# One of twelve streamed weight blocks is loaded over eight DMA engines in place of sixteen

## The chip, the cores and the metric

The kernel runs on one core of one Trainium2 chip. The core has a matrix engine (PE, with its weight loads shown apart as PEld), three elementwise engines (DVE, ACT, POOL), a queue engine (SP), and 16 DMA engines that all DMA queues share. The metric is device time in microseconds of one execution; lower is better. The kernel before takes 1960.46 us (median of three runs, 1957.11 to 1960.54).

## The reference: what is computed

Two independent parts, side by side in the last axis of the output. The weights and inputs are bf16.

```
# part A: attention over segments of 32 tokens with 8 memory rows that are carried along
for s in range(64):                                   # 2048 tokens / 32
    h = concat([mem, x[:, 32*s:32*s+32]])             # 40 rows of 1024
    q, k, v = h @ Wq, h @ Wk, h @ Wv                  # 32 heads of 128, so 1024 -> 4096 each
    p = softmax(where(mask, q @ k.T * 128**-0.5, -1e9))
    o = (p @ v) @ Wo                                  # 4096 -> 1024
    mem, out[s] = o[:8], o[8:]
# part B: a long convolution of u (2048 x 1024) with a kernel built from A, B, C, dt (128 states)
K = einsum('dn,dnl,dn->dl', C, exp(dt*A*l), dt*B).real
y = irfft(rfft(u) * rfft(K)) + u * Dskip
```

Each segment of part A needs the memory that the segment before it made, so the 64 segments run strictly one after the other, and each needs all four weight matrices, 32 MB in all. These do not fit on the chip.

## The kernel before

Part B runs first (about the first 600 us), with preparations for part A beneath it. Then comes the loop over the 64 segments (`for s in range(NS)`, L406), then one last product for the left-over rows (L656 to L670).

**Weight blocks.** A block is 128 rows (partitions) by 2048 bf16 columns, 512 KB, 4096 bytes in each partition. Wq, Wk and Wv have 16 blocks each, (matrix, chunk of 16 heads, one of eight slices of the 1024 inputs); Wo has 16, ("o", u), with two heads in each. Most stay in on-chip memory for the whole loop (`W_res`). Three are parked in other places (`KEPT`). Twelve are streamed: they are loaded again in every segment. They are listed by `STREAM` and `STREAM_O` (L26, L27): k chunk 0 block 2, q chunk 0 block 2, k chunk 1 blocks 1 and 5, q chunk 1 block 4, v chunk 0 blocks 2 and 7, v chunk 1 blocks 4 and 7, and o 4, 8 and 13. That is also the order of their use in a segment, so o 13 is the last of the twelve.

**Where they come from.** Before the loop, `streamed_copies` (L63) makes a private copy of each streamed block in DRAM (tiles `WD_k_...`, `WD_q_...`, `WD_v_...`, `WD_o_...`) of 128 rows by 2048 columns, by one DRAM to DRAM DMA for each (L69). The copies are issued one by one from SP inside part B (L1272).

**How they are loaded.** `unit(key)` (L300) hands out the block that a matmul needs. For a streamed block it calls `stage` (L337), which issues one DMA on SP's queue into one of four slots of the staging tile `wst` (`SLOTS = 4`, slots taken in turn). SP's instruction stream has nothing else in the loop, so it runs ahead of PE: the load of a block is issued as soon as PE has done with the block four places before it, which had the same slot. The first three loads are issued before the loop (L1709). ACT's queue has the small transfers: per segment one load of 128 KB (`PKd`, L376), one of 112 KB (`VXd`, L382), and two stores of 64 KB (`OLd`, L392, and the output rows, L396).

**Who uses them.** In `quads` (L407) each block of q, k or v is used by four matmuls into four column groups (L414). In `oproj` (L520) each block of Wo is used by eight matmuls (L527): blocks 0 to 4 first, then 5 to 7, then 8, 10, 12, 14, 9, 11, 13, 15. After block 13 comes only 15, then the output rows are turned (L627) and become the memory rows of the next segment (`hT`, L629).

**After the loop** the three streamed blocks of Wo are loaded once more (L647) for the last product, ahead of the left-over rows (`OLd`, L652), which are copied into place (L573) for the matmuls of L664.

The DMA semaphores count one step for each DMA engine that a transfer uses. Loads with other shapes that the prediction speaks of: `xb` (L121, 96 partitions of 2048 bytes), and the loads of `Kx` and `Kp` into `XM` and `k` in part B (L1095, 128 partitions of 1024 bytes).

Of the kernel before, what the change touches and what calls it, by code (L numbers as in the profile page):

```python
# [10 lines left out]
BF16 = mybir.dt.bfloat16  # L11
# [13 lines left out]

STREAM = {("k", 0): (2,), ("q", 0): (2,), ("k", 1): (1, 5), ("q", 1): (4,), ("v", 0): (2, 7), ("v", 1): (4, 7)}  # L26
STREAM_O = (4, 8, 13)  # L27

BANK = {("k", 0): "b0", ("q", 0): "b1", ("k", 1): "b2", ("q", 1): "b0", ("v", 0): "b3", ("v", 1): "b2"}
KEPT = {("k", 0, 7): (("K7a", 0, 512), ("K7b", 512, 512), ("K7c", 1024, 512), ("K7d", 1536, 384), (None, 1920, 128)),  # L30
# [28 lines left out]
def streamed_keys():  # L59
    return [key for key in [(m, t, kc) for (m, t), kcs in STREAM.items() for kc in kcs] + [("o", u) for u in STREAM_O]]  # L60


def streamed_copies(ctx, tc, src):  # L63
    nc = tc.nc
    dram = ctx.enter_context(tc.tile_pool(name="a_wd", bufs=1, space=bass.MemoryType.DRAM))
    out, copies = {}, []
    for key in streamed_keys():
        t_ = dram.tile([128, 2048], BF16, name="WD_%s" % "_".join(str(i) for i in key))
        copies.append(lambda t_=t_, key=key: nc.sync.dma_start(  # L69
            out=t_[:].rearrange("e (h d) -> e h d", h=2) if key[0] == "o" else t_[:], in_=src(key)))  # L70
        out[key] = t_
    return out, copies


class Ahead:
# [3 lines left out]
    def __init__(self, ctx, tc, x, src, seg_len):  # L79
        self.nc, self.tc, self.x, self.src = tc.nc, tc, x, src  # L80
        self.S, self.Dm = x.shape
        self.SL, self.XM = seg_len, 24
        self.XL, self.KC, self.NS = seg_len - 24, self.Dm // 128, self.S // seg_len
        dram = ctx.enter_context(tc.tile_pool(name="a_dram", bufs=1, space=bass.MemoryType.DRAM))
        self.VXd = dram.tile([self.NS + 1, 128, 256 + self.KC * self.XM], BF16, name="VXd")
        self.PKd = dram.tile([self.NS, 128, 512], BF16, name="PKd")
        self.PVd = [dram.tile([self.NS * self.XL, 2048], BF16, name="PVd%d" % t) for t in range(2)]
        self.OLd = dram.tile([self.NS // 8, 128, 8 * 256], BF16, name="OLd")
# [183 lines left out]
def part_a(ctx, tc, x, src, WD, HE, seg_len, out_a, ahead, W_res, rest, places, first):  # L272
    nc = tc.nc
# [26 lines left out]
    def unit(key):  # L300
        if key in rest:

            rest.remove(key)
            load_resident(tc, wres, src, key, W_res, None, places.pop(0)() if places else None)
        if key in W_res:
            return W_res[key]
        if key in KEPT:
            return ahead_of.pop(key) + halves.get(key, [])
        between.pop(key, lambda: None)()
        if key in first:  # L310
            return first.pop(key)
        if key[0] == "v":
            for k_ in rest[0:3 if key[1] == 0 else 1]:
                rest.remove(k_)
                load_resident(tc, wres, src, k_, W_res)
        return stage(key, WD[key][:])

    ctx_l = ctx_w.enter_context(ExitStack())
    pers = ctx_l.enter_context(tc.tile_pool(name="a_pers", bufs=1))
# [14 lines left out]
    def words(out, in_):  # L334
        nc.vector.tensor_scalar(out=out.bitcast(I32), in0=in_.bitcast(I32), scalar1=0, scalar2=None, op0=ALU.bitwise_or)  # L335

    def stage(key, in_):  # L337
        t_ = wst.tile([128, 2048], BF16, name="wst", tag="w%d" % (loads[0] % SLOTS))
        loads[0] += 1
        nc.sync.dma_start(out=t_[:].rearrange("e (h d) -> e h d", h=2) if len(in_.shape) == 3 else t_[:], in_=in_)  # L340
        return t_

    def load_kept(key):
# [62 lines left out]
    for s in range(NS):  # L406
# [123 lines left out]
        a = quads("k", 0, (0, 2, 4, 6, 1, 3, 5, 7))  # L530
        k0 = evac(a, "k0")
        a = quads("q", 0, range(0, 6))
# [4 lines left out]
        a = quads("k", 1, range(0, 3))  # L537
# [16 lines left out]
        a = quads("q", 1, range(KC))  # L554
# [3 lines left out]
        a = quads("v", 0, range(0, 3))  # L558
# [34 lines left out]
        a = quads("v", 1, range(0, 5))  # L593
# [46 lines left out]
    wo = {}  # L640
    for u in order:
        if ("o", u) in W_res:
            wo[u] = W_res["o", u]
        else:
            wo[u] = spare.pop(0)
            if ("o", u) in WD:
                nc.sync.dma_start(out=wo[u][:], in_=WD["o", u][:])  # L647
            else:
                nc.sync.dma_start(out=wo[u][:].rearrange("e (h d) -> e h d", h=2), in_=src(("o", u)))
    stores(NS - 1, ob)  # L650
# [6 lines left out]
    for b in range(4):  # L657
        pe = [ps_k.tile([128, 512], F32, name="pe", tag="keep%d" % (2 * (b % 2) + n)) for n in range(2)]
        for u in order:
            for hh in range(2):  # L660
                h = 2 * u + hh
                hi = 16 * (h // 16) + 4 * (h % 4) + (h % 16) // 4
# [983 lines left out]
@with_exitstack  # L1646
def kernel(
    ctx: ExitStack,
    tc: tile.TileContext,
    A_x: bass.AP,  # L1650
    A_mem0: bass.AP,
    A_Wq: bass.AP,
    A_Wk: bass.AP,
    A_Wv: bass.AP,
    A_Wo: bass.AP,
    A_seg_len: bass.AP,
    B_u: bass.AP,
    B_A_re: bass.AP,
    B_A_im: bass.AP,
    B_B_re: bass.AP,  # L1660
    B_B_im: bass.AP,
    B_C_re: bass.AP,
    B_C_im: bass.AP,
    B_log_dt: bass.AP,
    B_Dskip: bass.AP,
    out: bass.AP,
):
    seg_len = int(A_seg_len)
    Dm = A_x.shape[2]
    Db = B_u.shape[2]  # L1670
    out_a = out[0, :, 0:Dm]
    out_b = out[0, :, Dm:Dm + Db]
    src = weight_blocks(A_Wq.rearrange("d h e -> d (h e)"), A_Wk.rearrange("d h e -> d (h e)"),
                        A_Wv.rearrange("d h e -> d (h e)"), A_Wo.rearrange("h e d -> (h e) d"))
    WD, copies = streamed_copies(ctx, tc, src)
    ahead = Ahead(ctx, tc, A_x[0], src, seg_len)
    ctx_w = ctx.enter_context(ExitStack())
    W_res, places, first = {}, [], {}
    rest = Keys(RESIDENT)
    rest.ctx = ahead.ctx = ctx_w  # L1680

    def residents(stay, early, uqs, last):
        def put(t_):
            load_resident(tc, None, src, rest.pop(0), W_res, None, t_)
        for _ in range(EARLY[0]):
            load_resident(tc, stay, src, rest.pop(0), W_res)
            yield
        def some(where, tag, n):
            t_ = where.tile([128, n, 2048], BF16, name="W%d" % n, tag=tag)
            return [t_[:, i, :] for i in range(n)]  # L1690
        for t_ in some(stay, "KT1", 2):
            put(t_)
            yield
        for t_ in early:
            put(t_)
            yield
        put(last[0])
        yield
        for t_ in uqs:
            put(t_)  # L1700
            yield
        ahead.wst = ctx_w.enter_context(tc.tile_pool(name="a_wst", bufs=1, side="right"))
        pool = ctx_w.enter_context(tc.tile_pool(name="a_wre0", bufs=1, side="right"))
        for _ in range(EARLY[1]):
            load_resident(tc, pool, src, rest.pop(0), W_res)
            yield
        for i, key in enumerate([("k", 0, 7)] + streamed_keys()[0:SLOTS - 1]):
            first[key] = t_ = ahead.wst.tile([128, 2048], BF16, name="wst", tag="w%d" % i)
            tc.nc.sync.dma_start(out=t_[:], in_=WD[key][:] if key in WD else src(key))  # L1709
            yield  # L1710
        for i in [c // 2 for c in PAIRS]:
            places.append(lambda i=i: stay.tile([128, 2048], BF16, name="W1", tag="MI%d" % i))
        for i in range(LATE):
            put(places.pop(0)())
            yield
        put(last[1])
        yield

    low = low_blocks(ctx, tc)
    ahead.low = low.pop()  # L1720
    copies += [lambda t_=t_: load_resident(tc, None, src, rest.pop(0), W_res, None, t_) for t_ in low]

    def first_state(m0, xt):
        nc = tc.nc
        consts = constants(tc, ahead)
        hT = next(consts)
        nc.sync.dma_start(out=xt[:].rearrange("p k r -> p (k r)"), in_=ahead.VXd[0, :, 256:])
        nc.sync.dma_start(out=m0, in_=A_mem0[0])
        pm = yield
        for kc in range(8):  # L1730
            nc.tensor.transpose(out=pm[:, kc, :], in_=m0[:, kc * 128:(kc + 1) * 128], identity=ahead.consts[0][0:8, 0:8])
        nc.vector.tensor_copy(out=hT[:, :, ahead.XM:], in_=pm)
        nc.gpsimd.tensor_copy(out=hT[:, :, 0:ahead.XM], in_=xt[:])
        yield
        next(consts)
        yield

    with ExitStack() as ctx_b:
        part_b(ctx_b, tc, B_u[0], B_A_re, B_A_im, B_B_re, B_B_im, B_C_re, B_C_im, B_log_dt, B_Dskip, out_b, ahead, copies, residents, first_state)
    with ExitStack() as ctx_a:  # L1740
        part_a(ctx_a, tc, A_x[0], src, WD, A_Wo.shape[0] * A_Wo.shape[1], seg_len, out_a, ahead, W_res, rest, places, first)
# [35 lines left out]
```

## Time and profile before

| | us |
|---|---|
| median of three runs | 1960.46 (1957.11 to 1960.54) |
| profiled execution, span from first to last instruction | 1954.2 |
| part B and preparations | about 0 to 612 |
| loop over 64 segments | about 612 to 1890 |
| last product | about 1894 to 1954 |

| engine | busy us in the whole span | share |
|---|---|---|
| PE | 1810.2 | 93% |
| PEld | 1106.9 | 57% |
| DVE | 1379.4 | 71% |
| ACT | 934.7 | 48% |
| POOL | 443.1 | 23% |

PE's granted clock is full in the loop. The DMA engines moved 591.08 MB, 302 GB/s over the span. Four groups make up 768 of the DMA issues: the streamed loads of v (256), k (192), o (192) and q (128), 512 KB each.

How to read it: matmuls are pipelined and their ends are modelled, so a busy PE is not PE at its peak. The DMA share is the mean over 16 engines of the time in which they have a packet in work. A wait is put down to what ended last before the waiting instruction. A row of the chain of waits has the start, the duration and what it was; its DMA pieces run from the issue to the landing.

### The profile page before, as it was taken

To read this page: it belongs to the slowest core of one execution; us is meant where nothing else is said; L and a number is where in the kernel's file an instruction comes from. 1 tells how busy PE (TensorE), PEld (TensorE's weight loads), DVE (VectorE), ACT (ScalarE), POOL (GpSimd) and SP (SyncE) were. 2 spreads that over 40 slices of the span, in tenths; PEclk is the share of its full clock that TensorE was granted. 3 is DMA by queue.
4 is the path that set the end of the run, shared out by engine and by line. 5 is a ranking of instruction groups with operands and counts; after the bars stand their busy time and mean duration, and the time that the engine had idled before them with its cause. 6 is when DMAs were issued, how large, how long until landed. Compare 5 with 4: busy or idle time off the path is not lost.

```text
span 1954.2 us, 74192 instructions
## 1 busy us (share of the span) xinstructions
PE 1810.2 (93%) x31750; PEld 1106.9 (57%) x31788; DVE 1379.4 (71%) x3431; ACT 934.7 (48%) x1670; POOL 443.1 (23%) x855
## 2 busy tenths in 40 slices
PE   8999999887997899999999999999999999998998
PEld 3666666556775555555555555555555555555554
DVE  8599989889994566666676766676766676666650
ACT  8799989851122334344434443444444444444320
POOL 2364545223222111111111111111111111111120
PEclk8999999878998999999999999999999999999999
DMA  7889898867589999999999999999999999999991
GB/s 222 243 232 283 237 287 243 221 188 253 169 272 334 347 340 340 340 339 336 355 339 346 345 335 336 339 341 350 344 350 334 347 341 347 339 350 324 338 343 30
DMA packets 337342, 591.08 MB, mean 302 GB/s; under 512 B 94848, under 2 KB 211048, under 8 KB 334964
## 3 DMA queue, kind: packets, MB, share of 16 engines
q1 hardware_dynamic: 284824, 531.85, 79.9%
q10 hardware_dynamic: 45532, 29.57, 4.9%
q0 software_dynamic: 6656, 24.92, 3.5%
q8 instruction: 249, 4.08, 0.8%
q14 instruction: 81, 0.66, 0.1%
HBM read 528.78 MB, written 68.47 MB: 306 GB/s over the span
## 4 chain that ended last, share of the span: by engine, by line
PE 37%; DMA 27%; DVE 4%; issue 1%; ACT 1%; POOL 0%; SPq 0%; ACTq 0%; DVEq 0%; POOLq 0%
PE acc L414 20%; DMA wst<-WD_v 8%; PE pp L527 8%; DMA wst<-WD_o 7%; DMA wst<-WD_k 3%; DMA arena<-PKd 3%; DMA wst<-WD_q 3%; PE pe L664 3%; PE tr L425 2%; DMA out_dram<-arena 1%; DMA out_dram<-uu 1%; PE pv L495 1%; PE pv L499 1%; DVE arena L621 1%; PE sc L439 1%
## 5 line engine op out<-in xcount | busy, mean ns | idle before, releaser
L414 PEld LDWEIGHTS <-a_hT 128*32 128x32 bf16 x12352 | 328.4, 96 | 324.0 <-issue 64.0
L420 ACT CAST arena<-acc 128x512 bf16<-128x512 f32 x384 | 224.8, 585 | 404.3 <-PE acc L414 324.5
L414 PE MATMUL acc<-wst,a_hT 128*32 128x512 bf16 x2304 | 229.5, 382 | 34.2 <-DMA wst<-WD_v 22.9
L527 PEld LDWEIGHTS <-arena 128*32 128x32 bf16 x8256 | 216.1, 96 | 73.2 <-issue 49.3
L335 DVE TENSOR_SCALAR arena<-keep 128x256 int32<-128x256 int32 (+1 forms) x512 | 175.6, 395 | 28.1 <-PE acc L414 28.0
L428 POOL COPY arena<-arena 128x128 bf16<-128x128 bf16 x128 | 37.3, 292 | 683.0 <-DMA arena<-PKd 314.4
L414 PE MATMUL acc<-XM,a_hT 128*32 128x512 bf16 x2560 | 172.7, 380 | 0.0
L458 ACT ACTIVATE sc<-sc 128x160 f32<-128x160 f32 (+1 forms) x192 | 63.9, 333 | 127.6 <-DVE sc L455 127.6
L454 DVE TENSOR_REDUCE a_mx<-sc 128x4 f32<-128x160 f32 (+1 forms) x192 | 71.7, 374 | 74.7 <-PE sc L442 73.3
L197 PE MATMUL pro<-XM,wsl 128*128 128x512 bf16 x480 | 117.7, 383 | 5.3 <-DVE kst L206 2.2
L527 PE MATMUL pp<-W_o,arena 128*32 128x256 bf16 x3584 | 120.6, 273 | 0.1
L414 PE MATMUL acc<-W,a_hT 128*32 128x512 bf16 x1536 | 120.0, 384 | 0.0
L542 DVE COPY arena<-tr 128x512 bf16<-128x512 bf16 x64 | 27.2, 425 | 128.8 <-PE tr L425 128.8
L462 DVE TENSOR_REDUCE a_mx<-sc 128x4 f32<-128x160 f32 (+1 forms) x192 | 72.9, 379 | 55.3 <-ACT sc L458 54.9
L489 POOL TENSOR_TENSOR arena<-arena,a_BD 128x128 bf16<-128x128 bf16 x128 | 51.1, 399 | 231.1 <-DVE arena L472 229.7
L1266 DVE TENSOR_SCALAR nr<-ptt 128x456 f32<-128x456 int16 x128 | 80.4, 628 | 31.8 <-PE ptt L1244 29.0
L1258 ACT ACTIVATE E<-pa 128x648 bf16<-128x648 f32 x128 | 87.7, 712 | 18.1 <-PE pa L1250 16.0
L414 PE MATMUL acc<-wq,a_hT 128*32 128x512 bf16 x1024 | 92.2, 381 | 0.0
L414 PE MATMUL acc<-g,a_hT 128*32 128x512 bf16 x1024 | 90.4, 379 | 0.0
L1459 POOL TENSOR_TENSOR Bt<-ev 128x512 bf16<-128x512 f32 x32 | 55.7, 1760 | 150.2 <-DVE ev L1456 150.2
L621 ACT CAST arena<-pp 128x128 bf16<-128x128 f32 x64 | 17.0, 265 | 149.8 <-DVE arena L621 149.8
L425 PEld LDWEIGHTS <-arena 128*128 128x128 bf16 x1024 | 57.8, 98 | 54.4 <-issue 45.1
(339 smaller groups left out, 4071.3 us busy)
## 6 DMA issues: line engine op xcount, KB each, us to landing
wst<-WD_v SPq DMA_DIRECT2D x256, 512.0 KB
wst<-WD_k SPq DMA_DIRECT2D x192, 512.0 KB
wst<-WD_o SPq DMA_DIRECT2D x192, 512.0 KB
wst<-WD_q SPq DMA_DIRECT2D x128, 512.0 KB
Ud<-ux POOLq DMA_DIRECT2D x16, 1024.0 KB, 8.2
wq<-Ud SPq DMA_DIRECT2D x32, 512.0 KB
wsl<-in_A_Wk_dram SPq DMA_DIRECT2D x16, 512.0 KB
wsl<-in_A_Wv_dram SPq DMA_DIRECT2D x16, 512.0 KB
```

The lines of the kernel that those rows point to most:

```text
L197: nc.tensor.matmul(a[:], lhsT=w[:, kc, 128 * j:128 * j + 128], rhs=xTl[:, kc, :, :].rearrange("p s k -> p (s k)"), start=(kc == 0), stop=( ...
L335: nc.vector.tensor_scalar(out=out.bitcast(I32), in0=in_.bitcast(I32), scalar1=0, scalar2=None, op0=ALU.bitwise_or)
L414: nc.tensor.matmul(a[32 * g:32 * g + 32, o_:o_ + rhs.shape[1]], lhsT=hT[:, kc, :], rhs=rhs, start=(kc == 0), stop=(kc == KC - 1), tile_pos ...
L420: nc.scalar.copy(out=q, in_=a[:])
L425: nc.tensor.transpose(out=p[:, hl, :, :].rearrange("p a b -> p (a b)"), in_=q[:, 128 * hl:128 * hl + 128], identity=ident[:])
L454: nc.vector.tensor_reduce(out=m_, in_=x, axis=AX.X, op=ALU.max)
L458: nc.scalar.activation(out=flat(sc, i), in_=flat(sc, i), func=ACT.Exp, scale=scale)
L462: nc.vector.tensor_reduce(out=m_, in_=x, axis=AX.X, op=ALU.add)
L527: nc.tensor.matmul(po[32 * qt:32 * qt + 32, o_:o_ + rhs.shape[1]], lhsT=oT[:, h % 4, (h % 16) // 4, :], rhs=rhs, start=False, stop=(h == 3 ...
L664: nc.tensor.matmul(pe[n][:], lhsT=left[2 * b + hi // 16][:, 128 * (hi % 16):128 * (hi % 16) + 128], rhs=wo[u][:, 1024 * hh + 512 * n:1024 ...
L1258: sc.activation(out=T["E", r, e // 4][:, lo:lo + 8 * NE].rearrange("p (i c) -> p i c", i=2), in_=T.pop(("p", r, e))[:, :, 0:4 * NE], func= ...
L1266: v.tensor_scalar(out=T["n", r, e // 4][:, lo:lo + 8 * NT], in0=T.pop(("t", r, e))[:, 0:8 * NT].bitcast(I16)[:, 0:16 * NT:2], scalar1=floa ...
```

## The change

Block o 13 gets another layout in its private DRAM copy and another access pattern in its loads. Its copy is now a tile of 8 rows, each holding 16 of the 128 weight rows (64 KB) and a gap of 64 elements (128 bytes) behind them, so that the 8 rows can't be read as one run. A load reads it as 8 x 16 x 2048 where it read 128 x 2048, so its slowest dimension is 8: the transfer goes over eight DMA engines, 16 rows each, and not over sixteen with 8 rows each. The DMA that fills the copy has that form too. The other eleven blocks keep their layout, their loads and their order. The same loads are issued at the same places of the program (in `stage`, after the loop, and before it), now through a small class. The data and the arithmetic are the same.

```diff
+PORTIONS = {("o", 13): ((128, 8),)}
...
+PITCH = 64
...
+class Streamed:
+    def __init__(self, dram, nc, src, key):
+        self.nc, self.src, self.key, self.pieces = nc, src, key, []
+        lo = 0
+        for i, (rows, engines) in enumerate(PORTIONS.get(key, ((128, 16),))):
+            name = "WD_%s_%d" % ("_".join(str(j) for j in key), i)
+            each = rows // engines
+            if key in PORTIONS:
+                t_ = dram.tile([engines, each * 2048 + PITCH], BF16, name=name)
+                ap = t_[:, 0:each * 2048].rearrange("a (b f) -> a b f", f=2048)
+            else:
+                ap = dram.tile([128, 2048], BF16, name=name)[:]
+            self.pieces.append((lo, lo + rows, ap))
+            lo += rows
+        assert lo == 128
+    def copy(self):
+        for lo, hi, ap in self.pieces:
+            flat = ap if len(ap.shape) == 2 else None
+            w = self.src(self.key)[lo:hi]
+            if self.key[0] == "o":
+                w = w.rearrange("(a b) h d -> a b h d", a=ap.shape[0]) if flat is None else w
+                out = ap.rearrange("a b (h d) -> a b h d", h=2) if flat is None else ap.rearrange("e (h d) -> e h d", h=2)
...
+            self.nc.sync.dma_start(out=out, in_=w)
+    def load(self, t_):
+        for lo, hi, ap in self.pieces:
+            self.nc.sync.dma_start(out=t_[lo:hi, :], in_=ap)
...
 def streamed_copies(ctx, tc, src):
...
+    out = {key: Streamed(dram, tc.nc, src, key) for key in streamed_keys()}
+    return out, [w.copy for w in out.values()]
...
-        return stage(key, WD[key][:])
+        return stage(key)
...
-    def stage(key, in_):
+    def stage(key):
         t_ = wst.tile([128, 2048], BF16, name="wst", tag="w%d" % (loads[0] % SLOTS))
         loads[0] += 1
-        nc.sync.dma_start(out=t_[:].rearrange("e (h d) -> e h d", h=2) if len(in_.shape) == 3 else t_[:], in_=in_)
+        WD[key].load(t_)
         return t_
...
-                nc.sync.dma_start(out=wo[u][:], in_=WD["o", u][:])
+                WD["o", u].load(wo[u])
```

More of the change, by code (lines that the diff above doesn't have):

```diff
@@ L60, in streamed_keys @@
     return [key for key in [(m, t, kc) for (m, t), kcs in STREAM.items() for kc in kcs] + [("o", u) for u in STREAM_O]]
+PITCH = 64
[21 more added lines that the diff above has]
+                out = ap.rearrange("a b (h d) -> a b h d", h=2) if flat is None else ap.rearrange("e (h d) -> e h d", h=2)
+            else:
+                w = w.rearrange("(a b) f -> a b f", a=ap.shape[0]) if flat is None else w
+                out = ap
+            self.nc.sync.dma_start(out=out, in_=w)
+    def load(self, t_):
+        for lo, hi, ap in self.pieces:
+            self.nc.sync.dma_start(out=t_[lo:hi, :], in_=ap)
 def streamed_copies(ctx, tc, src):
-    nc = tc.nc
     dram = ctx.enter_context(tc.tile_pool(name="a_wd", bufs=1, space=bass.MemoryType.DRAM))
[L66 to L72, printed above, removed]
+    out = {key: Streamed(dram, tc.nc, src, key) for key in streamed_keys()}
+    return out, [w.copy for w in out.values()]
 class Ahead:
@@ L1708, in residents @@
             first[key] = t_ = ahead.wst.tile([128, 2048], BF16, name="wst", tag="w%d" % i)
-            tc.nc.sync.dma_start(out=t_[:], in_=WD[key][:] if key in WD else src(key))
+            if key in WD:
+                WD[key].load(t_)
+            else:
+                tc.nc.sync.dma_start(out=t_[:], in_=src(key))
             yield
```

## The prediction

> **What bounds the kernel now.** I read the page's slices first, then the stretch of the loop (about 612 to 1890 us, 64 segments), the queues in it, the chain of waits, and the waits for the staging tile.
>
> The slices of the page, forty of 48.9 us; the loop is slices 13 to 39:
>
> ```profile
> DMA  7889898867589999999999999999999999999991
> GB/s 222 243 232 283 237 287 243 221 188 253 169 272 334 347 340 340 340 339 336 355 339 346 345 335 336 339 341 350 344 350 334 347 341 347 339 350 324 338 343 30
> ```
>
> Busy time by stretch, for the whole loop and for one segment (PE, weight load, DVE, ACT, POOL, clock, DMA share, GB/s):
>
> ```profile
> 612.00:1890.00 1278.00, 1199.16 (x25539) 698.49 (x25540) 839.61 (x2618) 524.57 (x1149) 201.49 (x513) 0.99 0.96 342
> 1201.75:1221.66 19.91, 18.77 (x403) 10.92 (x402) 12.95 (x41) 8.20 (x19) 2.77 (x8) 1.00 0.93 329
> ```
>
> PE and the 16 DMA engines are both nearly full. Two and a quarter segments in the queue view (packets, MB, share of 16 engines) and its rate in forty slices of 1.125 us:
>
> ```profile
> GB/s 404 386 293 362 299 396 375 323 379 348 389 251 280 262 284 266 317 360 397 353 335 351 376 374 403 389 348 362 321 269 310 353 284 328 353 317 386 350 330 354
> ...
> q1 hardware_dynamic: 3915, 14.24, 88.0%
> q10 hardware_dynamic: 1385, 0.93, 6.5%
> q8 instruction: 8, 0.13, 1.2%
> q14 instruction: 2, 0.02, 0.1%
> ```
>
> The chain of waits in the same stretch, in order of time, and PE's idle time before matmuls of the staging tile, over the whole run (us, times):
>
> ```profile
> 1204.36 6.49 DMA wst<-WD_v
> ...
> 1222.32 7.23 DMA wst<-WD_q
> ...
> 1235.97 6.51 DMA wst<-WD_k
> ```
> ```profile
>   DMA wst<-WD_v: 22.9, 25
>   DMA wst<-WD_o: 8.8, 18
>   DMA wst<-WD_k: 6.4, 11
>   DMA wst<-WD_q: 4.3, 6
> ```
>
> The chain runs from a released slot through a 6 to 7 us load back to a matmul. Shown waits are only 42.4 us (0.66 us a segment) because the four slots pace themselves: each load is issued when PE frees the slot of four blocks before. I set the landing of each load (the semaphore steps, one for each DMA engine it uses) against the first matmul of its block, segments 5 to 61. Block 13 is issued, lands 5.32 us later (the fifteenth of its 16 engines after 4.93), and is used 0.15 us after landing; in 74% of segments within 0.2 us. No other block of the twelve has so little room (k1 of chunk 1 has 0.69 us, o 4 has 0.24). So what is added to block 13's landing goes to PE almost whole.
>
> The trace also has a record of every DMA packet. Between 700 and 1800 us a 4096-byte packet takes 159 ns in the median, the next on its engine starts 155 ns after it began, and the mean is 180 ns. The bound is therefore each engine's own pace, not the sum: slices reach 404 GB/s.
>
> How full is each engine? q1, q10 and the fetches make 95.8% of a 19.9 us segment, 19.1 us for the mean engine. The store of the output rows (L396) shows only four landings of its own, 32 packets of 512 bytes at 27 ns on each of four engines: 0.86 us on these, 0.22 in the mean. These four carry 19.1 + 0.64 = 19.7 us of 19.9, the other twelve some 18.9. Four engines are full, and they are among the eight of the change: at L1095 two loads with four landings each go ahead of one with eight, and of its eight, four land after 2.70 to 3.06 us and four after 5.69 to 6.48, behind the two. [...]
>
> **The change part by part.**
>
> Block 13's load in the loop, 64 times. 512 KB on 16 engines is 8 packets each, 8 x 155 ns = 1.24 us; on eight engines it is 16, 2.48 us. The eight lowest gain 1.24 us a segment, the eight highest lose it. The full four are among the gainers. The relief of the others is worth nothing where a block waits for its last engine.
>
> Do packets keep their pace? Each of eight engines now writes 16 neighbouring partitions. The trace has loads of this shape in small: Kx into XM and k (L1095), 1024-byte packets on four or eight engines, each with 32 or 16 neighbouring rows of the 128. By packet records, 364.5 to 366.5 us, the 1024-byte packets took 46 ns in the median (mean 50). From 488 to 489.25 us, with only such a load in flight, they took 61.5 in the mean (1.34 times 46). From 367 to 369.25 us, beside 16-engine loads of 4096-byte packets, they took 73.5 (1.60 times) and the neighbours 226 (1.42 times 159). So the extra is 0 to 0.60 of 16 x 155 ns = 2.48 us, that is 0 to 1.49 us; I take 0.45, 1.12 us, since the loop always has other loads in flight, as the slower row has, while the first row shows that it need not happen at all.
>
> [...]
>
> Against it I set 0.15 us of block 13's room and 0.15 of the 0.66 us of waits, as a longer stop at block 13 gives the three loads already queued time to land. Per segment 1.24 + 1.12 - 0.15 - 0.15 = 2.06 us; times 64 is 132 us.
>
> The issue on SP. L1095's loads held SP 582 ns in the median where L340's hold it 320, so 0.26 us more. SP's next issue (chunk 0 of k, 1.46 us later in the segment above) waits for a slot of PE's anyway: nothing, or 0.26 x 64 = 17 us if that cover went. Nothing else is queued on SP in the loop.
>
> The copy into the private DRAM tile (L69, at 286 to 317 us). 256 packets of 2048 bytes on eight engines in place of 16, 84 ns each in the row of xb's loads: at most 16 x 84 = 1.3 us more, read first at 636 us; 0 to 1.3, I take nothing. The 128-byte gap between engine shares moves no byte and I price it at nothing.
>
> The last load (L647) lands at 1897.2 us, and its matmuls come at 1903.9. The OLd loads behind it on the same engines move by 1.2 to 2.4 us; the copies made from them end 0.6 us before the second block of the last product starts. 0 to 1.8 us; I take 1.
>
> Sum: 133 us on the profiled 1954.2; the runs shown have a median of 1960.46, 6.3 us above that span. 1960.5 + 133 = 2093 us.
>
> **The rivals.**
>
> Only the packets (no crowding). Speaks for it the 46 ns of the first row. 1.24 - 0.30 = 0.94 us, times 64, plus 1: 2021 us.
>
> [...]
>
> No change. Either memory and not the engines sets the 342 GB/s, so that eight engines run faster while eight rest, or the load still goes over all 16: 1960 us. Against the first, the 155 ns that hardly any packet undercuts and slices of 404; against the second, Kx's third load, of the same form (8 x 16 rows), has eight landings of its own. [...]
>
> Faster. If the eight highest engines were the late ones, their 1.24 us would come off the blocks that wait for them. Half of the 42.4 us of waits is 21: 1939 us. It decides only from the point where the lowest eight have 1.24 us of room a segment; the mean engine has 4.2% of 19.9 = 0.8, and the lowest four 0.2. Speaks for it that the last landing moves about: after an instruction fetch one engine is 1 to 2 us late, and in most of these cases it is not one of the four that store the rows.
>
> **How the numbers follow.** Crowding in part 52% (2093; its own range 2060 to 2135, from factors 1.34 to 1.60 and 0.2 us more or less given back), only the packets 26%, full crowding 8%, no change 7%, faster 7%. The range that leaves out no change, faster and the far end of full crowding, some 18%, is 2000 to 2180. About 0.2% (4 us) is what runs of this kernel can tell from no change: faster 7%, within 6%, slower 87%.
>
> **What would show it.** Block 13's load should have eight landings of its own and eight at once; its landing should come 2 to 2.5 us later, with PE waiting there about 2 us a segment, 64 times; waits for the k and q blocks behind it should shrink. GB/s in the loop should fall to about 310 and the segment grow to some 21.9 us. Packets of 4096 bytes well above 159 ns while block 13 is in flight would confirm the crowding; 159 there would leave only 1.24. It is wrong if PE's wait at block 13 stays under 0.3 us or if the segment keeps 19.8 us.

## The result, and the profile after

The changed kernel takes 2244.09 us (median of four runs, 2227.24 to 2252.33) against 1960.5 us for the kernel before: ratio 1.1439, 95% interval 1.1388 to 1.1489, some 284 us slower. The profiled execution has a span of 2250.6 us (before: 1954.2). Lines have moved: L414 is now L446, L527 is L559, and the streamed loads are issued at L98.

The slices of the page after, forty of 56.3 us: granted PE clock, DMA share, rate.

```profile
PEclk8999998699988899999998989999999999989999
DMA  7989987676998889889888888988898888888992
GB/s 216 256 244 268 266 245 216 208 248 190 292 313 265 265 283 290 272 271 285 287 270 248 259 263 279 285 281 282 278 284 284 285 280 262 277 270 283 294 286 74
```

In the loop the rate is about 280 GB/s where it was 340, and the DMA share is 8 tenths where it was 9: the engines, once nearly full, now stand idle part of the time. The clock digits are the first surprise: the loop's slices show 9 and several 8, where they showed 9 throughout before; a slice with an 8 is a mean of stretches at full and at half clock (the run's clock records are 1.0 and 0.5 alone).

Busy time by stretch after (us; PE, weight load, DVE, ACT, POOL with their instructions; PE clock, DMA share, GB/s): from the first matmul of a staged block to the end of the last, and the first 6.4 us of one segment.

```profile
609.60:2189.70 1580.10, 1300.34 (x25656) 718.20 (x25649) 846.54 (x2633) 525.86 (x1152) 205.31 (x515) 0.92 0.89 279
1323.48:1329.85 6.37, 6.37 (x80) 2.62 (x80) 2.32 (x8) 1.24 (x3) 0.29 (x1) 0.67 0.70 222
```

The same stretch before:

```profile
608.90:1892.90 1284.00, 1203.36 (x25654) 701.24 (x25647) 844.04 (x2632) 525.83 (x1152) 201.80 (x514) 0.99 0.96 342
```

So the loop grew by 296.1 us: PE stands idle 199.1 us longer (279.8 against 80.6), and it is busy 97.0 us longer with the same matmuls. The second row of after shows why it is busy longer: at the start of this segment PE is busy without a break, at a clock of 0.67.

PE's idle time before matmuls of the staging tile after, whole run (us, times), and the costliest groups of PE after, one row for each shape (busy us, mean ns, idle before):

```profile
  DMA wst<-WD_o: 218.4, 99
  DMA wst<-WD_v: 23.0, 24
```
```profile
L446 PE MATMUL acc<-W_k,a_hT 128*32 128x512 bf16 x768 | 98.7, 574 | 0.0
L446 PE MATMUL acc<-Wlow,a_hT 128*32 128x512 bf16 x768 | 98.7, 573 | 0.0
L559 PE MATMUL pp<-wst,arena 128*32 128x256 bf16 x1536 | 80.9, 288 | 228.8 <-DMA wst<-WD_o 218.4 <-DVE arena L367 9.5 <-DVE a_mx L495 0.3
```

Waits for the Wo blocks went from 8.8 to 218.4 us; those for the k and q blocks behind them (6.4 and 4.3) are gone. The matmuls of W_k and Wlow, the first of a segment, took 379 and 383 ns before and take 574 and 573 now. The row of Wlow before:

```profile
L414 PE MATMUL acc<-Wlow,a_hT 128*32 128x512 bf16 x768 | 64.4, 383 | 0.4 <-DVE a_hT L629 0.4
```

One stop in full. PE's timeline after (start, us, operation, in brackets the idle time before it and what ended it), and the chain of waits in the same stretch:

```profile
1315.03 1.26 PE L559 MATMUL pp<-W_o,arena 128*32 128x256 bf16 x40
1321.44 0.62 PE L559 MATMUL pp<-wst,arena 128*32 128x256 bf16 x8 [5.15 <-DMA wst<-WD_o]
...
1323.48 0.62 PE L446 MATMUL acc<-Wlow,a_hT 128*32 128x512 bf16 x4
1323.88 0.65 PE L446 MATMUL acc<-wst,a_hT 128*32 128x512 bf16 x4
...
1327.71 0.41 PE L446 MATMUL acc<-wst,a_hT 128*32 128x512 bf16 x4
```
```profile
1310.48 10.92 DMA wst<-WD_o
1321.40 0.04 issue
1321.44 1.10 PE pp L559 x11
...
1337.36 10.23 DMA wst<-WD_o
```

Block 13 is issued at 1310.48 and lands 10.92 us later; PE is through with the blocks ahead of it at 1316.3 and stands for 5.15 us (the mean is 2.95). Four matmuls of the next segment's first blocks then take 0.62 to 0.65 us, until at 1327.71 the same four take 0.41 again.

The queues in 1300 to 1345 us after (packets, MB, share of 16 engines):

```profile
q1 hardware_dynamic: 2961, 10.86, 78.6%
q10 hardware_dynamic: 808, 0.54, 3.9%
```

Read as time per packet, q1's 78.6% of 16 x 45 us over 2961 packets is 191 ns each; the prediction's rows of before give 88.0% of the same over 3915, 162 ns. Fewer packets fit, and each holds its engine longer.

The records of landings and of single packets say the same for the mean of segments 5 to 61. "At 159" is the share of 4096-byte packets of at most 165 ns, among those of all loads between 1.5 us after block 13's issue and its landing. "Half clock" is the time with a granted clock of 0.5, from the loop's first matmul of a staged block to its last. The rows below the second are the experiments.

| kernel | block 13, issue to landing, us | PE stands before it, us | segment, us | packet in flight, mean ns | at 159 | half clock in the loop, us |
|---|---|---|---|---|---|---|
| before | 5.32 | none | 19.69 | 194 | 89% | 17 |
| after | 9.08 | 2.95 | 24.26 | 254 | 36% | 266 |
| e1 16 engines x 8 neighbouring rows | 7.12 | 0.73 | 20.94 | 232 | 38% | 34 |
| e2 four loads of 8 x 4 | 7.63 | 2.22 | 22.27 | 220 | 55% | 157 |
| e3 two loads of 16 x 4 | 6.35 | 0.38 | 20.27 | 222 | 48% | 20 |
| e4 after, wait filled with matmuls | 8.95 | 0.56 | 23.06 | 248 | 36% | 34 |
| e5 after, wide gap in the copy | 8.92 | 3.08 | 23.85 | 252 | 36% | 241 |
| e6 before, padded copy | 5.36 | none | 19.84 | 191 | 89% | 17 |
| e11 loads of 8 x 12 and 8 x 4 | 8.24 | 2.48 | 23.11 | 226 | 46% | 188 |
| e12 four loads of 16 x 2 | 7.04 | 0.64 | 21.20 | 233 | 44% | 48 |
| e7 before + extra packets, DRAM to DRAM | 6.13 | 0.57 | 20.24 | 180 | 91% | 34 |
| e13 before + extra packets, rows 0 to 63, two loads | 6.04 | 0.74 | 20.47 | 187 | 90% | 38 |
| e14 before + extra packets, rows 64 to 127, two loads | 7.29 | 1.25 | 21.79 | 225 | 47% | 85 |
| e15 before + extra packets, rows 0 to 63, one load | 7.57 | 1.29 | 21.84 | 213 | 50% | 89 |

Block 13's load has sixteen landings before, at 3.36 to 5.32 us after the issue (means), and nine in the changed kernel: one record at 1.04 us, and eight at 6.62 to 9.08 us.

### The profile page after: what moved, and what is told of

Its sections match the earlier page's. It is cut to its first block, busy times and chain, and to the rows that moved or that the text cites. A ratio compares the mean times of both kernels' runs of the same rounds, so it can differ in the third digit from the quotient of the medians.

```text
span 2250.6 us, 74230 instructions
## 1 busy us (share of the span) xinstructions
PE 1910.3 (85%) x31788; PEld 1124.3 (50%) x31788; DVE 1379.8 (61%) x3431; ACT 935.2 (42%) x1670; POOL 445.4 (20%) x855
## 4 chain that ended last, share of the span: by engine, by line
PE 37%; DMA 35%; DVE 1%; issue 0%; ACT 0%; SPq 0%; ACTq 0%; DVEq 0%
PE acc L446 27%; DMA wst<-WD_o 26%; DMA wst<-WD_v 8%; PE pe L696 2%; PE pp L559 2%; PE tr L457 2%; PE tro L659 1%; DVE arena L653 1%; PE sc L471 1%; PE yp L1543 1%; DMA wst<-WD_k 0%; DMA out_dram<-uu 0%; PE hps L1543 0%; DMA a_half<-in_A_Wq_dram 0%; ACT arena L653 0%
## 5 line engine op out<-in xcount | busy, mean ns | idle before, releaser
L446 PEld LDWEIGHTS <-a_hT 128*32 128x32 bf16 x12352 | 336.8, 103 | 392.8 <-issue 137.9
L559 PEld LDWEIGHTS <-arena 128*32 128x32 bf16 x8256 | 222.5, 98 | 301.4 <-issue 277.1
L559 PE MATMUL pp<-wst,arena 128*32 128x256 bf16 x1536 | 80.9, 288 | 228.8 <-DMA wst<-WD_o 218.4
L446 PE MATMUL acc<-wst,a_hT 128*32 128x512 bf16 x2304 | 241.4, 408 | 24.2 <-DMA wst<-WD_v 23.0
L653 DVE CAST arena<-pp 128x128 bf16<-128x128 f32 x64 | 18.6, 291 | 260.7 <-PE pp L559 260.7
L446 PE MATMUL acc<-XM,a_hT 128*32 128x512 bf16 x2560 | 172.4, 381 | 0.0
L229 PE MATMUL pro<-XM,wsl 128*128 128x512 bf16 x512 | 124.4, 387 | 3.7 <-DVE XM L144 2.2
L559 PE MATMUL pp<-W_o,arena 128*32 128x256 bf16 x3584 | 124.0, 277 | 0.5 <-issue 0.5
L446 PE MATMUL acc<-W,a_hT 128*32 128x512 bf16 x1536 | 118.0, 383 | 0.0
L1298 DVE TENSOR_SCALAR nr<-ptt 128x456 f32<-128x456 int16 x128 | 80.3, 627 | 30.5 <-PE ptt L1276 27.5
L446 PE MATMUL acc<-W_k,a_hT 128*32 128x512 bf16 x768 | 98.7, 574 | 0.0
L446 PE MATMUL acc<-Wlow,a_hT 128*32 128x512 bf16 x768 | 98.7, 573 | 0.0
```

Source lines behind the costliest of these rows:

```text
L229: nc.tensor.matmul(a[:], lhsT=w[:, kc, 128 * j:128 * j + 128], rhs=xTl[:, kc, :, :].rearrange("p s k -> p (s k)"), start=(kc == 0), stop=( ...
L446: nc.tensor.matmul(a[32 * g:32 * g + 32, o_:o_ + rhs.shape[1]], lhsT=hT[:, kc, :], rhs=rhs, start=(kc == 0), stop=(kc == KC - 1), tile_pos ...
L559: nc.tensor.matmul(po[32 * qt:32 * qt + 32, o_:o_ + rhs.shape[1]], lhsT=oT[:, h % 4, (h % 16) // 4, :], rhs=rhs, start=False, stop=(h == 3 ...
L653: (nc.scalar.copy if j else nc.vector.tensor_copy)(out=osb[:, 128 * j:128 * j + 128], in_=pp[:, 1, 128 * j:128 * j + 128])
L1298: v.tensor_scalar(out=T["n", r, e // 4][:, lo:lo + 8 * NT], in0=T.pop(("t", r, e))[:, 0:8 * NT].bitcast(I16)[:, 0:16 * NT:2], scalar1=floa ...
```

## The experiments

**Is it the copy's layout?** e5 widens the gap in the changed kernel's copy from 128 bytes to 4224; e6 gives the kernel before a copy whose rows have a gap, still 128 rows over 16 engines.

```diff
-PITCH = 64
+PITCH = 2112
```
```diff
-        t_ = dram.tile([128, 2048], BF16, name="WD_%s" % ...)
+        t_ = dram.tile([128, 2048 + 64 * (key == ("o", 13))], BF16, name="WD_%s" % ...)[:, 0:2048]
```

> The changed kernel with a gap of 4224 bytes in place of 128 behind each engine's 64 KB in the private copy, so that the eight engines read from other offsets. Crowding where the block is written: nothing changes, 2225 to 2255 us. The layout of the private copy slows the reads: the time falls by 50 us or more, towards 2100.

> The kernel before, with 128 bytes behind every row of block 13's private copy; the load reads 128 rows of 4096 bytes over sixteen engines as before. Crowding where the block is written: as before, 1955 to 1970 us. Padded reads are slow: 2000 to 2080 us, as with the sixteen engines of eight neighbouring rows (2039.88).

Measured: e5 2231.54 us, ratio 1.1378 [1.1335, 1.1421]; e6 1957.77, 0.9985 [0.9966, 1.0004]. Neither gap matters, so the price is not in the gaps of the copy but in how the load is shared out.

**What does the unequal share alone cost?** e7 keeps block 13 as it was and puts one DRAM to DRAM transfer of 256 KB over eight engines ahead of it in each segment: eight engines get eight packets more, as in the change, but none of them goes to on-chip memory.

```diff
+        if key == ("o", 13):
+            nc.sync.dma_start(out=extra[0][:, 0:8 * 2048].rearrange("a (b f) -> a b f", f=2048),
+                              in_=WD[key][:].rearrange("(a b) f -> a b f", a=8)[:, 0:8, :])
```

> The kernel before, with one more DMA per segment, issued on SP ahead of block 13's load: 256 KB from DRAM to DRAM over eight engines, 8 packets of 4096 bytes on each, written nowhere on chip and used by nothing. It prices the eight extra packets an engine without the neighbouring rows. Unequal share costs the packets' own time, 1.24 us a segment less 0.3: 2010 to 2050 us. If the share costs nothing until rows crowd: 1960 to 1975 us. If DRAM to DRAM packets take much longer than 155 ns, more than 2050, to be read beside their durations.

Measured: 1991.14 us, 1.0153 [1.0118, 1.0189], +30 us or 0.47 us a segment. This lies between the two expected ranges. 91% of packets stay at 159 ns. Eight packets of 155 ns on "full" engines should have cost 0.94 us by the prediction's sum (1.24 less the 0.30 given back); they cost half of that, and block 13 lands 0.81 us later, not 1.24.

e8 aimed at the same point from the other side: in the kernel before, the store of the output rows, put down to four engines, is cut into four stores.

```diff
-            nc.scalar.dma_start(out=rows, in_=ob[:, 0, :])
+            for q in range(4):
+                nc.scalar.dma_start(out=rows[q], in_=ob[32 * q:32 * q + 32, 0, :])
```

> The kernel before, with the store of the output rows, which uses four engines, cut into four stores over sixteen engines. If four engines are full and pace the loop, as the prediction reads it, the loop loses up to 0.6 us a segment: 1920 to 1950 us. If they don't, or if three more issues on ACT delay its next copy out of PSUM: 1955 to 2000 us.

Measured: 2013.11 us, 1.0287 [1.0256, 1.0318]. This is above both expected ranges, and it says nothing of the four engines: ACT now waits 104.5 us for its stores of OLd before it writes its copies, so the longer queue on ACT spoils the comparison.

**How do other forms of block 13's load do?** Each is one line of the changed kernel, (rows, engines) for each load, in order:

```diff
-PORTIONS = {("o", 13): ((128, 8),)}
+PORTIONS = {("o", 13): ((128, 16),)}            # e1
+PORTIONS = {("o", 13): ((32, 8),) * 4}          # e2
+PORTIONS = {("o", 13): ((64, 16),) * 2}         # e3
+PORTIONS = {("o", 13): ((96, 8), (32, 8))}      # e11
+PORTIONS = {("o", 13): ((32, 16),) * 4}         # e12
```

> Block 13 goes over sixteen engines again, 8 packets each, but in the padded layout, so that each engine may write 8 neighbouring partitions. Crowding (engines that write neighbouring partitions get in each other's way): packets of block 13 slow down though no engine has more of them, its landing moves from 5.3 us to 6 or 7, time 1985 to 2080 us. Unequal share alone (eight extra packets an engine): as before, 1960 us. Layout of the private copy (padded rows read slower): late as well, 1985 to 2080.

> Block 13 goes over the eight engines in four loads of 32 rows, 4 rows an engine in each, so that an engine still has 16 packets but at any time the eight are on eight different groups of 4 partitions. Crowding: most of the delay goes, the landing is 1.2 to 2 us later than before in place of 3.8, time 2010 to 2080 us. Unequal share alone: the packets an engine has are the same, so 2220 to 2260 us. Three further issues on SP at about 0.6 us each should cost nothing, or up to 1.8 us a segment.

> Block 13 goes over sixteen engines in two loads of 64 rows, 4 rows an engine, 8 packets an engine in all, padded layout. [...] Unequal share alone: 1960 to 1970 us. Layout of the copy: like the run with four loads, whatever that one shows.

| form | median us | ratio |
|---|---|---|
| e1, 16 x 8 neighbouring rows | 2039.88 | 1.0405 [1.036, 1.0451] |
| e2, four loads 8 x 4 | 2133.43 | 1.0883 [1.0824, 1.0942] |
| e3, two loads 16 x 4 | 2001.73 | 1.0208 [1.0164, 1.0251] |
| e11, 8 x 12 and 8 x 4 | 2161.91 | 1.1035 [1.0989, 1.1081] |
| e12, four loads 16 x 2 | 2055.84 | 1.0497 [1.0457, 1.0538] |

e1 is the most telling: all 16 engines, 8 packets each as before, only with neighbouring rows on one engine. It costs 80 us, and its packets in flight are at 159 ns only 38% of the time, against 89%. That is crowding without any unequal share, with a somewhat later start of its packets in it (see e9). e2 was a miss: it was expected at 2010 to 2080, as each of its loads spreads eight engines over different rows. The last of the four is issued 2.11 us after the first, which explains part of it, but 45% of its packets are slow too. e3's 2001.73 us lie above the 1960 to 1970 expected of the unequal share alone, and 48% of its packets are at 159 ns.

**Loads by themselves.** e9 and e10 leave the whole computation out and run each form eight times in a row into one tile.

> Leaves out the whole computation: only loads of 4096-byte rows from DRAM into one tile on chip, eight of each form, one at a time, nothing else in flight. Forms (engines x neighbouring rows of each): 16 x 8 as the kernel before reads them, 8 x 16 as in the change, 16 x 8 neighbours as in the run with sixteen, then 2 x 16, 2 x 32, 4 x 16, 8 x 4, 16 x 4. [...] Rival, neighbouring rows are slow only beside other loads: 159 ns in every form. Rival, an engine is slow by itself when it walks over many rows: 2 x 16 slow like 8 x 16.

> Leaves out the whole computation, as the run with loads alone. [...] Rival, slowing grows with the number of rows of an engine or of engines: 8 x 12 and 4 x 24 slow like 8 x 16 or little less.

Measured, 4096-byte packets after each engine's first three (mean ns, share at 159; engines x rows of each). A packet's record doesn't name its engine, which is inferred from the packets' times, so another way to infer it moves some of these shares by up to about ten points. The loads of the first row ran beside the copies that prepare the other forms; the others ran alone.

| form | e9 | e10 |
|---|---|---|
| 16 x 8 as before | 169, 92% | |
| 16 x 8 neighbouring | 231, 25% | |
| 8 x 16 | 205, 36% | 208, 34% |
| 8 x 12 | | 161, 95% |
| 8 x 8 | | 168, 88% |
| 8 x 4 | 159, 100% | |
| 4 x 16, 4 x 24, 4 x 32 | 186, 67% (4 x 16) | 164, 97% (4 x 24); 183, 70% (4 x 32) |
| 6 x 16 | | 177, 75% |
| 2 x 16, 2 x 32 | 172, 92%; 186, 71% | 188, 65% (2 x 32) |
| 16 x 4 | 174, 71% | 169, 81% |

Block 13's form slows its packets with no other form in flight. Neither the number of engines nor that of rows decides: 8 x 12 moves 96 rows at 161 ns and 4 x 24 the same at 164, while 4 x 16 is at 186. So the rival of e10 fails for these two forms. For 2 x 32 the runs differ little (186 and 188 ns). Which forms are clean was not explained, but it led to the guess that e11, made of the two clean forms 8 x 12 and 8 x 4, would run clean in the loop, and that e12 would.

These loads show something else: SP takes longer to issue such a load, and its packets start later. In e9 the issue of an 8 x 16 load takes 567 to 634 ns, and its first packet starts 1.34 us after the issue began (median). The one plain load with nothing ahead of it took 319 ns to issue, and its first packet started after 0.95 us. In the loop block 13's issue takes 599 ns in place of 320 (medians), so some 0.4 us of its later landing is this later start, by an estimate from e9.

> [...] Rival, any neighbouring rows or any load on eight engines is slow: 2200 us or more.

> [...] It prices the three further issues on SP without unequal share or crowding, beside the run with four loads over eight engines (2133.43). Theory: issue at 0.32 us each puts the last quarter some 1 us later, 1980 to 2030 us, so that the rest of that run's 173 us is the unequal share and its longer issues; if the issues cost more than 2 us, 2080 or more and that run said little of crowding.

Measured: 2161.91 us for e11, near the 2200 of its rival, and 2055.84 for e12, between its two ranges, with 46% and 44% of packets at 159. e11's forms, clean alone, are not clean beside the other blocks' loads. So the next guess was that it counts which rows the packets write while other loads are in flight.

**Which rows are written.** To tell this apart, the kernel before keeps block 13's load, and extra loads ahead of it put eight more packets on each of eight engines, always 256 KB, rewriting rows of a resident block with the values they hold. The edit of e13, with e14's and e15's differences:

```diff
+EXTRA = (0, 32)                 # e14: (64, 96)
...
+        if key == ("o", 13):
+            for lo, e_ in extra:     # e_: 8 x 4 rows; e15: one load, 8 x 8 rows, EXTRA = (0,)
+                nc.sync.dma_start(out=W_res["k", 1, 0][lo:lo + 32, :], in_=e_)
```

e13 writes rows 0 to 63, in two loads with four rows an engine in each, e14 rows 64 to 127 in the same form, and e15 rows 0 to 63 again, in one load with eight neighbours an engine. The packet records name neither engine nor row, so which engine writes which row is not shown; the three runs compare prices.

> The kernel before, with two more loads per segment ahead of block 13's, each of 32 rows over eight engines, 4 rows an engine: rows 0 to 31 and 32 to 63 of a resident block are written again with what they hold. Each of the eight engines gets eight extra packets. [...] If the extra packets slow here as well: 2060 us or more.

> The same with rows 64 to 95 and 96 to 127 of that block: the same engines, the same number of packets, the same issues. [...] Rival, only the number of packets on the eight engines counts: within 15 us of that run.

> The same eight extra packets on each of the eight engines as one load of rows 0 to 63, 8 neighbouring rows an engine. [...]

Measured: e13 1995.88 us, 1.0196 [1.0154, 1.0238]; e14 2097.29, 1.0703 [1.0642, 1.0763]; e15 2091.4, 1.0658 [1.0598, 1.0717]. e14 lies 101 us above e13, not within the 15 of its rival. PE's idle time before matmuls of the staging tile in e13, then in e14:

```profile
  DMA wst<-WD_o: 54.9, 69
```
```profile
  DMA wst<-WD_o: 117.7, 114
```

And their queue q1 in 1300 to 1345 us, e13 first:

```profile
DMA packets 5262, 15.85 MB, mean 352 GB/s; under 512 B 578, under 2 KB 1602, under 8 KB 5252
...
q1 hardware_dynamic: 4124, 14.95, 91.4%
```
```profile
DMA packets 4779, 14.07 MB, mean 313 GB/s; under 512 B 523, under 2 KB 1547, under 8 KB 4773
...
q1 hardware_dynamic: 3645, 13.22, 86.8%
```

As many engines, same bytes, same number of packets, same place in the queue, and private copies of the same form, so what is read doesn't differ: only the rows that are written do. In e13 the packets keep 159 ns (90%), the stretch moves 352 GB/s, and the loop pays 38 us. Some 19 of these are the two issues, not the packets: they take SP 0.65 us each, and block 13 is issued 0.34 us after its slot is free, where it is 0.04 in the kernel before. e14 has the same delay (0.36), so it doesn't touch the comparison. In e14 the loop pays 139, with q1 at 171 ns a packet against 160 in this stretch. e15 rules out that the upper rows are slow in themselves: rows 0 to 63, dealt out otherwise, cost 134, with block 13 issued without delay (0.04).

**What does the half clock cost?** e4 is the changed kernel with twelve matmuls of 512 columns whose result is not used ahead of block 13's, so that PE doesn't stand still while it waits.

```diff
+                if u == 13:
+                    fill = ps.tile([128, 512], F32, name="fill", tag="b2")
+                    for _ in range(FILL):                      # FILL = 12
+                        nc.tensor.matmul(fill[:], lhsT=ident[:], rhs=W_res["o", 12][:, 0:512], start=True, stop=True, skip_group_check=True)
```

> The changed kernel with 12 extra matmuls of 128 x 512 (0.21 us each, 2.6 us) into an unused accumulator just ahead of block 13's wait; their results are not used. Theory that PE's clock falls because PE stands idle in that wait: matmuls of the next segment's first block go from 0.62 us to 0.40 for four, the mean granted clock from 0.92 to about 0.97, and some 70 us come back, 2160 to 2190 us, with block 13 landing as late as before. Rival, that these matmuls are slow for another reason (the loads in flight beside them): 2230 to 2270 us.

Measured: 2182.0 us, 1.1125 [1.1075, 1.1175], 62 us less than after, with more work done. Groups of PE in e4, as above:

```profile
L447 PE MATMUL acc<-Wlow,a_hT 128*32 128x512 bf16 x768 | 65.9, 392 | 0.0
L559 PE MATMUL fill<-W_o,a_ident 128*128 128x512 bf16 x704 | 173.5, 380 | 3.4
```

The first block's matmuls are back at 392 ns (383 before, 573 after), while block 13 lands as late as in after (8.95 against 9.08 us). So some 62 of the 284 us (14 more or less, by the two intervals) are a second cost, set off by the stop and not by the transfer: half clock in the loop falls from 266 to 34 us.

## Why the prediction was right and wrong

**Right.** The direction, and where it comes from: block 13's load has eight landings of its own (and one record at 1.04 us, where the forecast had eight at once), it lands later, PE waits for it in nearly every segment, and the waits for the k and q blocks behind it are swallowed (10.7 us to nothing). Two prices near nothing held: the gap (e5, e6), and the last load, as the stretch behind the loop took 60.9 us where it took 61.3. Of what was to be seen, the rate of about 310 GB/s (279) and the segment of 21.9 us (24.26) went further the same way than foretold.

**The issue on SP was not quite nothing.** The prediction asked only what waits behind the longer issue, and that held. But block 13's own packets start some 0.4 us later (the estimate from e9), some 25 us in 64 segments.

**The term of 1.24 us for the extra packets was too large.** It stood on "four engines are full". e7 and e13 add just these eight packets and pay 30 and 38 us, 0.47 and 0.59 us a segment, of which e13's later issue is 0.30. Block 13 lands 0.81 us later after its issue in e7 and 0.72 in e13, not 1.24. The mean DMA share and the reading of the row store left no room; by these two landings the engines had 0.4 to 0.5 us (1.24 less 0.81 and 0.72, an estimate). No record names an engine: that the four of the row store are among the eight of the load was my reading, and "lowest" and "highest" are names for the eight in it and the eight outside it.

**The term of 1.12 us for crowding was much too small.** This is the step that failed. I took a factor of 0.45 between 0 and 0.60, from small loads of part B, and charged it to block 13's own 16 packets. In the loop, packets in flight with block 13 take 254 ns in the mean in place of 194, and these include the other blocks' packets on the same engines. An estimate: if the last engine is busy from the first packet (0.95 and 1.34 us after the issue, from e9) to the landing, then 4.37 us at 194 ns is 22.5 packets before, and 7.74 us at 254 ns is 30.5 after: 8 packets more, as many as the change adds. The landing's 3.76 us are then 0.39 us for the later start, 8 x 254 ns = 2.0 us for the extra packets, and 22.5 x 60 ns, nearly 1.4 us, for the slowing of all that were there already. The last part had no place in the sum, although the row with 226 ns neighbours (1.42 x 159) had been read. The two causes cost more together than apart: block 13 lands 1.80 us later in e1, which has the crowding and the later start without extra packets, and 0.72 in e13, which has the extra packets without crowding: 2.52 of the 3.76. No run shows the factor behind the 8% of "full crowding", every packet of block 13 at twice its time: of the packets in flight a quarter is at 309 ns or more, half at 205 or less.

**The waits given back were about right, and a second block was missed.** Block 13's 3.76 us and the 1.15 us at half clock (below) make 4.91 us, and the segment grew by 4.57, so 0.34 was given back where I had 0.30. Block 8 of Wo, loaded just ahead, also lands 0.70 us later (6.08 against 5.38), and PE stands 0.44 us longer before it. That is the slowing of the neighbours: block 8 lands 1.09 and 1.06 us later in e1 and e14, but only 0.12 later in e7 and e13.

**A whole step was missing: the clock.** The prediction took PE to run at full clock after its wait. In after, PE's stop at block 13 is followed by half clock, mostly for 3.41 us (49 of the run's 72 spells), sometimes for twice that (16); the loop has 266 us of it where it had 17. From a segment's first matmul of the staged k block to that of the staged q block (chunk 0) PE takes 3.11 us in place of 1.96, which is 1.15 x 64 = 74 us, and PE's busy time in the loop is 97.0 us longer in all. e4 gets 62 us back. From the forecast: the landing came 3.76 us later where I had added up 2.36, and the missing 1.40 us are 90 us in 64 segments; 133 + 90 + 62 makes 285 against the measured 284. So the landing that was mis-sized and the clock that was left out account for the time, though a sum of means and medians is this close only by luck.

**The rivals.** "Only the packets" is refuted by e13 against e14 and by the packet records; "no change" and "faster" by the result. For "faster" the condition was 1.24 us of room in the eight engines of the load; block 13's landing in e7 and e13 shows 0.4 to 0.5 of it, which is not enough, and crowding would have spent it anyway.

**What stays open.** Why the rows count. e13 to e15 show that the price goes with the rows that are written and with how they are dealt out (38, 139 and 134 us); which engine writes which row is in no record here, so no rule of which rows collide is shown. Nor do the runs say why 8 x 16 alone runs most of the earlier packets of an engine (the third to the seventh) at 159 ns and slows after, why 2 x 32 alone slows about a third of its packets, or how much of e2's and e12's loss is crowding and how much the later issue of their last load. That the later start of e9 holds in the loop as well is an estimate.

## What to carry to other kernels

Here a DMA that shared its rows out differently from the loads in flight beside it slowed them as well as itself (packets in flight 254 ns in place of 194, block 8's landing 0.70 us later): price all packets that wait on those engines, not its own alone, and keep streamed loads in one form unless a run shows that it does no harm. When a change makes PE stand for a few microseconds once per loop turn, add the half clock after the stop to the bill; matmuls without use in the wait bought 62 of 284 us back here. A mean DMA share of 95% does not mean that an engine has no room: adding eight packets by themselves measures it (e7: 0.47 us a segment for 1.24 us of packets).

## What the hardware showed that was not expected

The clock fell after short stops, which the prediction had left out. Over eight kernels (before, after, e1, e2, e5, e11, e12, e14), segments sorted by how long PE stood before block 13, with the share in which half clock followed:

| PE stood, us | segments | half clock follows | Wlow matmuls of the next segment, mean ns |
|---|---|---|---|
| under 0.5 | 107 | 0% | 383 |
| 0.5 to 1 | 84 | 2% | 385 |
| 1 to 1.5 | 33 | 18% | 425 |
| 1.5 to 2 | 44 | 36% | 464 |
| 2 to 2.5 | 66 | 67% | 519 |
| 2.5 to 3 | 50 | 88% | 565 |
| 3 to 3.5 | 48 | 92% | 604 |
| over 3.5 | 40 | 85% | 578 |

There is no edge, but a slope from 1 to 3 us. The stop is not all of PE's idle time there: in after, PE also stands 0.50 us in the 3.4 us ahead of it and 0.18 us between it and the next segment (means). Gaps of 2 to 2.5 us are followed by half clock in two of three segments here.

And the same bytes on as many engines differ in price 3.5 times and more by the rows they go to: 38 us for rows 0 to 63 in two loads (19 of them the later issue), 134 for the same rows in one load, 139 for rows 64 to 127. About 27 of the 101 us between e13 and e14 are the clock again: PE's busy time in the loop is 1208.43 us in e13 and 1235.50 in e14.
